# One attention unit's probabilities turned on TensorE for three of four head pairs, and a higher planned price for a DMA of turned blocks

## The chip, the cores and the metric

The kernel runs on one core of one Trainium2 chip. The metric is device time in microseconds (us) of one execution, taken as the median of several timed runs. The engines of the core are TensorE (PE in the profile, with PEld for its weight loads), VectorE (DVE), ScalarE (ACT), GpSimd (POOL) and SyncE (SP), whose queue issues all DMA transfers of this kernel.

## What is computed

Attention with a few global keys and a local window, four sequences of 768 positions, eight heads of 64, and on its output a gated feed-forward layer:

```python
B, H, S, D = q.shape                                   # 4, 8, 768, 64
scores = (1.0 / np.sqrt(D)) * np.matmul(q, k.transpose(0, 1, 3, 2))
rel = pos[:, None] - pos[None, :]
is_global = pos[None, :] < n_global                    # 8
is_local = (rel >= 0) & (rel < n_local)                # 96
dist = np.where(is_global & ~is_local, n_local, np.abs(rel))
scores = np.where(is_global | is_local, scores - slopes * dist, -1e9)
a = softmax(scores)                                    # over the keys
x = np.matmul(a, v)                                    # to [3072, 512]
out = ((x @ w_a) * (x @ w_b)) @ w_out                  # [512, 1536] twice, [1536, 512]
```

All of it is float32.

## The kernel before, in words

**Units.** The 3072 rows are 24 blocks of 128, and these are dealt out to eight units of 4, 2, 3, 3, 3, 3, 3 and 3 blocks (UNITS). A unit has an attention and a feed-forward part. While TensorE works on the feed-forward part of unit u, the attention of unit u+1 is woven in between. Names carry the unit: p15_4 is the second projection (1) of unit 5 for the fourth-numbered piece of the 1536 hidden columns, acc5_0 an output block of unit 5, ps6_3_2 the scores of unit 6, head 3, block 2, and pa6_1 the attention output of unit 6, head pair 1. "Third unit" is unit 2, whose attention lies beside the feed-forward part of unit 1, the shortest of them, with two blocks.

**Feed-forward** (moe, L934 on). For each of twelve pieces of 128 hidden columns: proj makes 24 matmuls into p0 and p1 (each product is three matmuls of split halves, L970), DVE multiplies the two (L1009), ACT and DVE split the result, and back makes nine matmuls (six for two blocks) into acc (L988). In unit 0 the weights are also converted and split on ACT and DVE (load_w), each piece shortly before its first use.

**Attention of units 2 to 7** (attention, L875 on). For each of the 24 pairs of head and block that a unit has: two score matmuls (L902); on DVE the bias and the row minimum (L608); on ACT the exponential and its sum (L624); on DVE two small steps (L639, L646); then the division (L656 on ACT or L658 on DVE). The probabilities must then be turned, since the product with v needs them by keys. Here DVE transposes squares of 32 by 32 (blocks32, L699) into one shared buffer tp, and swap issues 16 DMAs (L713) that move the squares of a whole head pair to their places in pf. The 20 or 24 matmul records with v (values, L730; the profile shows two for each instruction) write pa, and ACT copies it out. tp lies over the wm tile, so the profile calls it wm. tp and pf exist once each.

**Attention of units 0 and 1** (quad). There turn (L673 on) transposes 128 by 128 on TensorE with an identity matrix (L683) into PSUM, and ACT or DVE copies the result to pf or back to t (L410, L412).

**The order.** No instruction has a place written by hand. Each step is recorded as an Op with a due time, what it reads and writes, and a cost on each engine that may run it; Schedule.order then plays a simple machine with these costs, and the order in which steps start there becomes the order on each queue. A swap's 16 DMAs are 16 Ops of cost 480 (ns, dma=480) on the SP queue, and a reader of a DMA's result becomes ready 2300 after its end there (LAGS), plus spare (SPARE = 200 for values). For everything due before the end of unit 1, search tries 400 random shifts of the due times and keeps the best. SLACK says how many of the twelve pieces before the end of a feed-forward part the next attention is due to end: 3.0.

```python
            due = start + (2 * c + 2) * step
            self.swap(due, pf, slot)
            pa = self.bank("psA", f"pa{u}_{c}")
            self.values(due, pl, range(pl.nb), v, probs, pa)
```

Of the kernel before, what the change touches and what calls it, by code (L numbers as in the profile page):

```python
# [25 lines left out]
P = 128  # L26
# [8 lines left out]
PAIRED = 2  # L35
# [4 lines left out]
CHUNKS = 12  # L40
SQ = 32

START = 52000
WLEAD = 6000
LOADLEAD = 8000
SPLITLEAD = 3000
SLACK = 3.0
BACKLOG = 1.0


SPARE = 200.0
PRICE = {"dve": 2.0, "pool": 2.0}


# [155 lines left out]
class Schedule:  # L210
# [16 lines left out]
    def op(self, due, emit, reads=(), writes=(), spare=0.0, port=(), **costs):  # L227


        self.ops.append(Op(len(self.ops), due, costs, emit, reads, writes, spare, port))  # L230
# [18 lines left out]
    def order(self, ops, dues):  # L249
# [28 lines left out]
        def wins(op, e):  # L278
# [3 lines left out]
            for o, c in op.costs.items():  # L282
                at[o] = max(free[o], now) + c * PRICE.get(o, 1.0)
                for due, index, other in ready[o]:
# [77 lines left out]
def pe(n, m=P):  # L362
    return max(n / 2.23 + 2.5, m / 1.2)
# [5 lines left out]
class Fast:  # L369
# [300 lines left out]
                act=act(w) + 100,  # L670
            )

    def turn(self, due, wins, t, pt, pf):  # L673

        nc = self.nc
        starts = []
        for o, w in wins:
            starts += [o] if w == P else [o, o + w - P]
        n = len(starts) * P

        def emit(e):
            for c, o in enumerate(starts):
                nc.tensor.transpose(pt[:, c * P : c * P + P], t[:, o : o + P], self.ident)  # L683

        self.plan.op(due, emit, [t], [pt], pe=len(starts) * 112)
        self.copy(due, lambda: pf[:, :n], lambda: pt[:, :n], n, [pt], [pf], psum=True)

    def blocks32(self, due, w, t, slot, n):

# [14 lines left out]
    def swap(self, due, pf, m):  # L704

        nc, tp, n = self.nc, self.tp, CHUNKS * SQ
        for a in range(P // SQ):
            for b in range(P // SQ):
                out = lambda a=a, b=b: pf[SQ * b : SQ * b + SQ, a * n : a * n + m * SQ]
                src = lambda a=a, b=b: tp[SQ * a : SQ * a + SQ, b * n : b * n + m * SQ]  # L710
                self.plan.op(
                    due,
                    lambda e, out=out, src=src: nc.sync.dma_start(out(), src()),  # L713
                    [tp],
                    [(pf, (a, b))],
                    dma=480,
                )

    def values(self, due, pl, blocks, v, probs, pa):
# [19 lines left out]
        n = sum(len(pl.vslot[i]) for i in blocks)  # L739
        self.plan.op(due, emit, reads, [pa], pe=n * 218 + 290, spare=SPARE if pl.late else 0.0)  # L740

# [133 lines left out]
    def attention(self, u, start, end):  # L875
        nc, pl, op = self.nc, PLANS[u], self.plan.op

        x = [(self.raw0, WIDE + c * MAXQ) for c in range(2)]
        x += [(self.sbuf([P, MAXQ], F32, f"x{c}", f"x{u}_{c}"), 0) for c in range(2, NCC)]
        if u < PAIRED:  # L880
            self.second(x, start, end)
            return x
        step = (end - start) / H
        for c in range(NCC):
            probs = {}
            v = self.fetch_v(u, c, start + (2 * c + 1) * step - LOADLEAD)
            pf = self.sbuf([P, CHUNKS * P], F32, "pf", f"pf{u}_{c}", 1)
            slot = 0
            for s in range(2):
                h = 2 * c + s  # L890
                due = start + h * step
                raw = self.fetch(u, h, due - LOADLEAD)
                qh, ql, kk = self.split(u, h, due - SPLITLEAD, raw)
                for i in range(pl.nb):
                    due = start + h * step + (i + 1) * step / pl.nb
                    k0, w = pl.kwin[i]
                    n = f"{u}_{h}_{i}"
                    ps = self.bank(("psS", "psT")[(pl.nb * h + i) % 2], "ps" + n)

                    def scores(e, i=i, k0=k0, w=w, ps=ps, qh=qh, ql=ql, kk=kk):  # L900
                        for m, q in enumerate((qh, ql)):
                            nc.tensor.matmul(  # L902
                                ps[:, :w],
                                q[:, i * P : i * P + P],
                                kk[:, k0 : k0 + w],
                                start=m == 0,
                                stop=m == 1,
                            )

                    op(due, scores, [qh, ql, kk], [ps], pe=2 * pe(w))  # L910
                    turn = (pl.nb * h + i) % (TBUFS + len(self.spares))
                    if turn < TBUFS:
                        t = self.sbuf([P, 2 * P], F32, "t", "t" + n, TBUFS)
                    else:
                        t = self.spares[turn - TBUFS]
                    sm = self.sbuf([P, 8], F32, "sm", "sm" + n, 6)
                    self.softmax(h, due, [(0, w)], ps, t, sm, [(self.wm, k) for k in range(MBUFS)])
                    chunks = len(pl.vslot[i])
                    self.blocks32(due, w, t, slot, chunks)

                    def get(k, slot=slot, pf=pf):
                        view = pf[:, :].rearrange("p (a m i) -> p m a i", a=P // SQ, m=CHUNKS)
                        return view[:, slot + k]

                    probs[s, i] = (pf, get)
                    slot += chunks
            due = start + (2 * c + 2) * step
            self.swap(due, pf, slot)
            pa = self.bank("psA", f"pa{u}_{c}")
            self.values(due, pl, range(pl.nb), v, probs, pa)  # L930
            self.result(u, c, due, pa, x)
        return x
# [115 lines left out]
    def run(self):  # L1048
        self.open()
        t = START  # L1050
        x = self.first(t - 3000)
# [6 lines left out]
        def ahead(u, t):  # L1058
            xs[u] = self.attention(u, t, t + (NF - SLACK) * steps[u - 1])

# [385 lines left out]
```

## Time and profile before

| | |
|---|---|
| median of 3 runs | 772.8 us (771.91 to 773.62) |
| profiled execution | 769.24 us |
| its span, first to last instruction | 767.5 us |
| PE busy | 719.2 us (94%) |
| DVE busy | 456.4 us (59%) |
| ACT busy | 398.8 us (52%) |
| DMA queue of the kernel | 73.70 MB, 30.5% of 16 engines |

All times of the trace count from the first instruction. A busy time is the union of an engine's instructions; an idle time before an instruction is put down to what came last of what it waited for. PE is an engine with one queue in order: an instruction that waits holds up all behind it.

### The profile page before, as it was taken

What the parts mean: (1) busy time and instruction counts of PE and PEld (TensorE: products, weight loads), DVE (VectorE), ACT (ScalarE), POOL (GpSimd) and SP (SyncE); (2) the same over time, 40 slices, a digit from 0 to 9 for tenths busy, and PEclk for the clock granted to TensorE, in tenths of its full rate; (3) what the DMA queues carried; (4) which work ended last, traced back from release to release, by engine and by line L of the source; (5) the groups of instructions that cost most, each with busy time, mean ns of one, the idle gap of its engine ahead of it and who ended that gap; (6) DMA issues with size and microseconds to landing.
All of it is one profiled execution on the core that took longest, in us unless ns stands there. A gap on an engine that the chain in (4) does not pass through costs nothing.

```text
span 767.5 us, 12583 instructions
## 1 busy us (share of the span) xinstructions
PE 719.2 (94%) x4344; PEld 643.1 (84%) x4344; DVE 456.4 (59%) x1476; ACT 398.8 (52%) x983; POOL 12.7 (2%) x34
## 2 busy tenths in 40 slices
PE   5799999999898999999989999999899999999996
PEld 4568777798888988898879888898888988889996
DVE  6999999867772664465636656266562666322111
ACT  6999877556562653455525456255452655321111
POOL 1000000000000000000000000000000000000000
PEclk9989999999999999999999999999999999999999
DMA  7878010133452133222332333313232232210001
GB/s 285 354 308 353 20 32 30 48 105 97 112 141 84 56 98 100 69 61 83 91 99 82 81 99 96 87 59 82 85 102 69 87 104 61 54 57 8 1 1 45
DMA packets 38520, 74.57 MB, mean 97 GB/s; under 512 B 8497, under 2 KB 21041, under 8 KB 38449
## 3 DMA queue, kind: packets, MB, share of 16 engines
q1 hardware_dynamic: 38448, 73.70, 30.5%
q8 instruction: 36, 0.59, 0.3%
q14 instruction: 36, 0.29, 0.1%
HBM read 50.07 MB, written 6.29 MB: 73 GB/s over the span
## 4 chain that ended last, share of the span: by engine, by line
PE 46%; SPq 26%; DVE 12%; DMA 6%; issue 5%; ACT 4%; DVEq 0%; ACTq 0%
SPq L713 26%; PE p L970 25%; PE acc L988 13%; DMA pf<-wm 6%; PE pa L730 4%; DVE wm L699 2%; DVE kk L420 2%; DVE ql L576 1%; PE ps L777 1%; DVE t L608 1%; PE ps L902 1%; DVE wm L608 1%; PE pt L683 1%; ACT t L624 1%; DVE kk L412 1%
## 5 line engine op out<-in xcount | busy, mean ns | idle before, releaser
L970 PE MATMUL p<-xh,wt 128*128 128x384 f32 (+2 forms) x1488 | 419.1, 339 | 2.7 <-DVE wt L412 1.7
L970 PEld LDWEIGHTS p<-xh,wt 128*128 128x128 f32 x1488 | 271.1, 189 | 17.5 <-issue 3.0
L970 PE MATMUL p<-xl,wt 128*128 128x384 f32 (+2 forms) x816 | 270.5, 341 | 0.5 <-DVE xl L837 0.3
L988 PE MATMUL acc<-wt,hh 128*128 128x512 f32 x576 | 205.3, 397 | 0.0
L970 PEld LDWEIGHTS p<-xl,wt 128*128 128x128 f32 x816 | 153.7, 189 | 10.1 <-DVE xl L837 0.6
L1009 DVE TENSOR_TENSOR raw<-p,raw 128x384 f32<-128x384 f32 (+2 forms) x96 | 53.2, 554 | 136.3 <-PE p L970 123.1
L988 PEld LDWEIGHTS acc<-wt,hh 128*128 128x128 f32 x576 | 108.8, 189 | 21.8 <-issue 2.1
L988 PE MATMUL acc<-wt,hl 128*128 128x512 f32 x288 | 113.6, 394 | 0.0
L410 ACT COPY raw<-p 128x384 f32<-128x384 f32 (+2 forms) x96 | 45.8, 477 | 105.5 <-PE p L970 103.6
L410 ACT CAST hh<-raw 128x384 fp32r<-128x384 f32 (+2 forms) x87 | 44.1, 507 | 56.6 <-DVE raw L1009 55.9
L730 PE MATMUL pa<-pf,v 128*64 128x128 f32 x640 | 43.1, 278 | 30.8 <-DMA pf<-wm 24.9
L730 PEld LDWEIGHTS pa<-pf,v 128*64 128x64 f32 x640 | 35.8, 138 | 40.4 <-issue 33.0
L624 ACT ACTIVATE t<-t,sm 128x232 f32<-128x232 f32 (+2 forms) x120 | 57.1, 480 | 20.3 <-DVE sm L608 19.2
L420 DVE TENSOR_TENSOR hl<-raw,hh 128x384 fp32r<-128x384 f32 (+2 forms) x96 | 53.1, 553 | 19.9 <-ACT hh L410 19.4
L988 PEld LDWEIGHTS acc<-wt,hl 128*128 128x128 f32 x288 | 54.5, 189 | 7.4
L608 DVE CUSTOM_DVE_ANT_0 t<-ps,rel 128x232 f32<-128x232 f32 (+1 forms) x100 | 39.0, 399 | 34.1 <-PE ps L902 32.3
L656 ACT ACTIVATE t<-t,sm 128x232 f32<-128x232 f32 (+2 forms) x86 | 40.4, 485 | 21.0 <-DVE sm L646 16.8
L699 DVE STREAM_TRANSPOSE wm<-t 128x256 f32<-128x256 f32 (+1 forms) x72 | 25.7, 399 | 42.4 <-DMA pf<-wm 39.8
L624 ACT ACTIVATE wm<-wm,sm 128x232 f32<-128x232 f32 (+2 forms) x72 | 34.2, 476 | 18.7 <-DVE sm L608 18.3
L656 ACT ACTIVATE wm<-wm,sm 128x232 f32<-128x232 f32 (+2 forms) x57 | 26.9, 477 | 28.7 <-DVE sm L646 21.1
L420 DVE TENSOR_TENSOR kk<-raw,kk 64x348 fp32r<-64x348 f32 (+1 forms) x82 | 38.5, 470 | 2.5
L902 PE MATMUL ps<-kk,ql 128*128 128x128 f32 (+1 forms) x144 | 39.4, 275 | 0.0
(86 smaller groups left out, 671.6 us busy)
## 6 DMA issues: line engine op xcount, KB each, us to landing
wr<-wts SPq DMA_DIRECT2D x24, 768.0 KB, 10.2
pf<-wm SPq DMA_DIRECT2D x192, 48.0 KB, 1.9
raw<-qkv SPq DMA_DIRECT2D x24, 366.0 KB, 3.1
pf<-wm SPq DMA_DIRECT2D x192, 40.0 KB, 1.9
raw<-qkv SPq DMA_DIRECT2D x24, 314.0 KB, 3.0
v<-qkv SPq DMA_DIRECT2D x16, 384.0 KB, 3.1
out<-o SPq DMA_DIRECT2D x23, 256.0 KB, 2.1
v<-qkv SPq DMA_DIRECT2D x16, 256.0 KB, 2.6
```

Of the source, the lines that this page charges most:

```text
L410: self.nc.scalar.copy(out(), src())
L420: lambda e: self.engine(e).tensor_sub(out(), a(), b()),
L608: lambda e, j=j, o=o, w=w, neg=neg: nc.vector.tensor_tensor_reduce(t[:, o : o + w], ps[:, o : o + w], neg[:, :w], -(2.0 ** -(h + 1)), 3.0e ...
L624: lambda e, j=j, o=o, w=w: nc.scalar.activation(t[:, o : o + w], t[:, o : o + w], AF.Exp, bias=sm[:, j : j + 1], scale=-1.0, accum_out=sm[ ...
L656: nc.scalar.mul(t[:, o : o + w], t[:, o : o + w], r)
L699: nc.vector.transpose(dst, src)
L713: lambda e, out=out, src=src: nc.sync.dma_start(out(), src()),
L730: nc.tensor.matmul(pa[D * s : D * s + D, i * P : i * P + P], v[:, v0 : v0 + D], probs[s, i][1](c), start=c == 0, stop=c == len(slots) - 1,)
L902: nc.tensor.matmul(ps[:, :w], q[:, i * P : i * P + P], kk[:, k0 : k0 + w], start=m == 0, stop=m == 1,)
L970: nc.tensor.matmul(p[:, :T], wt(), b[:, b0 : b0 + T], start=c == 0 and n == 0, stop=c == NCC - 1 and n == 2,)
L988: nc.tensor.matmul(acc[i][:, :], hs[:, i * P : i * P + P], wt(), start=f == 0 and n == 0, stop=f == NF - 1 and n == 2,)
L1009: lambda e, asb=asb, pb=pb: nc.vector.tensor_mul(asb[:, :T], pb[:, :T], asb[:, :T]),
```

## The change

Four things change.

1. In swap each of the 16 DMAs is planned at SWAP = 640 in place of 480. This is a number of the plan alone; the DMAs are the same.
2. SLACK becomes 3.5: the attention of each unit is due half a piece earlier.
3. In unit 2 (SHORT), for the head pairs 0, 2 and 3 (OLD), the six probability blocks of a pair are not transposed by DVE and moved by 16 DMAs, but by TensorE with turn: for each head and block one or two 128 by 128 transposes into bank psT, and a copy to pf. That is ten transposes and six copies a pair. Pair 1 of unit 2 and all pairs of units 3 to 7 keep blocks32 and swap.
4. The scores of these three pairs all use bank psS, where they alternated between psS and psT. turn's Op gets a spare of 200 and writes part of pf from column p0 on.

```diff
+SHORT = PAIRED
+OLD = (0, 2, 3)
...
-SLACK = 3.0
+SLACK = 3.5
...
+SWAP = 640.0
...
-        self.plan.op(due, emit, [t], [pt], pe=len(starts) * 112)
-        self.copy(due, lambda: pf[:, :n], lambda: pt[:, :n], n, [pt], [pf], psum=True)
+        self.plan.op(due, emit, [t], [pt], pe=len(starts) * 112, spare=spare)
+        out = lambda: pf[:, p0 : p0 + n]
+        self.copy(due, out, lambda: pt[:, :n], n, [pt], [(pf, p0)], psum=True)
...
-                    dma=480,
+                    dma=SWAP,
...
+            old = u == SHORT and c in OLD
...
-                    ps = self.bank(("psS", "psT")[(pl.nb * h + i) % 2], "ps" + n)
+                    ps = self.bank(("psS", "psT")[not old and (pl.nb * h + i) % 2], "ps" + n)
...
-                    self.blocks32(due, w, t, slot, chunks)
-
-                    def get(k, slot=slot, pf=pf):
+                    if old:
+                        pt = self.bank("psT", "pt" + n)
+                        self.turn(due, [(0, w)], t, pt, pf, slot * P, SPARE)
+                    else:
+                        self.blocks32(due, w, t, slot, chunks)
+
+                    def get(k, slot=slot, pf=pf, old=old):
+                        if old:
+                            return pf[:, (slot + k) * P : (slot + k + 1) * P]
...
-            self.swap(due, pf, slot)
+            if not old:
+                self.swap(due, pf, slot)
```

Since all instructions are placed by the plan, nearly every place moves a little. Three places follow. The lines of the changed file are a few higher: L902 becomes L909, L970 L984, L988 L1002, L730 L736, L683 L688, L420 L425, L608 L613.

**Place 1, TensorE, a head pair with a swap (unit 6, pair 1).** First before, from the last scores of the pair (ps6_3_2) to its product with v (pa6_1):

```order
L902 MATMUL ps6_3_2_5878<-kk6_3_5665,qh6_3_5663 128x232
L902 MATMUL ps6_3_2_5878<-kk6_3_5665,ql6_3_5673 128x232
L970 MATMUL p15_4_5835<-xh5_5481,wt4_1_933 128x384
...
L988 MATMUL acc5_0_5626<-wt5_1_1015,hl5_5_6003 128x512
L988 MATMUL acc5_0_5626<-wt5_1_1015,hh5_5_5993 128x512
L730 MATMUL pa6_1_6060<-pf6_1_5940,v6_1_5459 64x128 x10
L988 MATMUL acc5_1_5633<-wt5_1_1015,hh5_5_5993 128x512
```

and now:

```order
L909 MATMUL ps6_3_2_5832<-kk6_3_5665,qh6_3_5663 128x232
L909 MATMUL ps6_3_2_5832<-kk6_3_5665,ql6_3_5673 128x232
L984 MATMUL p05_4_5826<-xh5_5481,wt4_0_913 128x384
...
L984 MATMUL p15_6_6031<-xl5_5491,wt6_1_1098 128x384
L984 MATMUL p15_6_6031<-xh5_5481,wt6_1_1098 128x384
L736 MATMUL pa6_1_6058<-pf6_1_5909,v6_1_5465 64x128 x10
...
L909 MATMUL ps6_5_2_6079<-kk6_5_5850,qh6_5_5848 128x232
```

Between the scores and the product with v there stood 82 matmuls: 51 of L970, 21 of L988 and 10 of scores. Now there are 104: 66 of L970 (now L984), 18 of L988 (now L1002), 10 of scores, and the 10 instructions of the pair before, pa6_0.

**Place 2, TensorE, the third unit, pair 0.** Before, its block transposes stand on VectorE, between steps of the feed-forward part of unit 1:

```order
L658 TENSOR_SCALAR wm_505<-wm_505,sm2_1_2_1721 128x232
L639 TENSOR_SCALAR sm2_2_0_1756<-sm2_2_0_1756 128x1
L699 STREAM_TRANSPOSE wm_505<-wm_505 128x2x4x32
L420 TENSOR_TENSOR hl1_1_1794<-raw0_88,hh1_1_1782 128x256
L646 RECIPROCAL sm2_2_0_1756<-sm2_2_0_1756 128x1
```

Now the same block (head 1, block 2) is turned on TensorE, pt2_1_2, a few matmuls ahead of the pair's product with v:

```order
L984 MATMUL p11_2_1793<-xh1_1579,wt2_1_741 128x256
L688 MATMUL pt2_1_2_1823<-ident_93,wm_440 128x128 x2
L984 MATMUL p01_3_1827<-xh1_1579,wt3_0_830 128x256
L984 MATMUL p01_3_1827<-xl1_1594,wt3_0_830 128x256
...
L909 MATMUL ps2_2_1_1844<-kk2_2_1690,ql2_2_1725 128x256
L736 MATMUL pa2_0_1849<-pf2_0_1615,v2_0_1253 64x128 x10
```

The 16 DMAs of the pair are gone from the SP queue, the transposes are on TensorE's, and the copies to pf are on ACT's and DVE's.

**Place 3, VectorE, the weights of unit 0's piece 5.** wt5_0 is the first half of that piece's weights; its last write is a TENSOR_TENSOR (L420, now L425). Before:

```order
L498 ISA wm_505<-wr5_0_585,wm_505 128x1536
L459 TENSOR_SCALAR wm_505<-wm_505 128x768
L608 ISA t0_1_1_0_978,sm0_1_1_0_979<-ps0_1_1_0_926,rel_70 128x232
...
L420 TENSOR_TENSOR wt5_0_976<-wm_505,wt5_0_976 128x768
L479 SCALAR_TENSOR_TENSOR wm_505<-wr5_1_630,wm_505 128x768
```

and now:

```order
L503 ISA wm_440<-wr5_0_588,wm_440 128x1536
L484 SCALAR_TENSOR_TENSOR wm_440<-wr5_1_631,wm_440 128x768
...
L503 ISA wm_440<-wr5_1_631,wm_440 128x1536
L1023 TENSOR_TENSOR raw0_88<-p10_4_960,raw0_88 128x512
...
L425 TENSOR_TENSOR wt5_0_997<-wm_440,wt5_0_997 128x768
```

The write stood in row 224 of VectorE's order and stands in row 240: two steps for the piece's second half and a multiplication of the feed-forward part have come ahead of it. Its first reader on TensorE (the first matmul of piece 5) is row 292 in both.

More of the change, by code (lines that the diff above doesn't have):

```diff
@@ L671, in softmax, with turn @@
             )
-    def turn(self, due, wins, t, pt, pf):
+    def turn(self, due, wins, t, pt, pf, p0=0, spare=0.0):
         nc = self.nc
```

## The prediction

> **What bounds the kernel now.** I read the page first, then the busy times by stage, then who TensorE waited for. The page:
>
> ```profile
> span 767.5 us, 12583 instructions
> PE 719.2 (94%) x4344; PEld 643.1 (84%) x4344; DVE 456.4 (59%) x1476; ACT 398.8 (52%) x983; POOL 12.7 (2%) x34
> ```
>
> TensorE is busy for 94%, so it is the bound, and the time can only fall by its idle 48 us or by less work on it. Busy time by stage (start, unit 0, unit 1, units 2 to 6, unit 7; the columns are the length, then the busy time and count of PE, PEld, DVE, ACT and POOL, the granted clock, the DMA share and GB/s):
>
> ```profile
> 0.00:60.00 60.00, 46.84 (x305) 34.24 (x306) 49.98 (x183) 51.90 (x129) 2.51 (x20) 0.91 0.82 320
> 60.00:160.00 100.00, 99.88 (x511) 79.35 (x510) 95.97 (x204) 74.65 (x146) 0.00 (x0) 1.00 0.25 86
> 160.00:228.00 68.00, 63.97 (x492) 58.59 (x491) 48.80 (x196) 39.72 (x116) 2.33 (x3) 1.00 0.41 116
> 228.00:690.00 462.00, 436.76 (x2664) 404.05 (x2663) 248.25 (x874) 218.74 (x566) 7.88 (x11) 1.00 0.29 82
> ```
>
> Idle are 13.2 us at the start, 0.1 in unit 0 (where DVE is full as well), 4.0 beside unit 1 and 25.2 after that. TensorE's waits name the last two:
>
> ```profile
> PE pa L730 <- DMA pf<-wm: 24.9, 21, 2.0
> ...
> PE pa L730 <- issue: 3.9, 3, 2.1
> ```
>
> That is 24 waits, one for each head pair of units 2 to 7, all ahead of the product with v: 28.8 us, 1.2 each. (The three put down to "issue" stand at the same instruction.) Why TensorE comes too early is seen in the SP queue and in TensorE's timeline, here for two pairs:
>
> ```profile
> 482.82 10.02 SPq L713 DMA_DIRECT2D pf<-wm  x16
> ...
> 538.51 11.56 SPq L713 DMA_DIRECT2D pf<-wm  x16
> ```
> ```profile
> pf<-wm SPq DMA_DIRECT2D x192, 48.0 KB, 1.9
> ```
> ```profile
> 494.46 1.53 PE L730 MATMUL pa<-pf,v 128*64 128x128 f32 x24 [0.81 <-issue]
> ...
> 551.75 1.31 PE L730 MATMUL pa<-pf,v 128*64 128x128 f32 x20 [2.01 <-DMA pf<-wm]
> ```
>
> Sixteen issues take 10.0 us (0.63 each), at worst 11.6, and the last lands 1.9 us after its issue. The plan before counts 16 x 0.48 + 2.3 + 0.2 (the spare of values) = 10.2 us from the first issue to the product with v. The second pair shows 551.75 - 538.51 = 13.2 us; the first, which is the usual case, 10.0 - 0.6 + 1.9 = 11.3 to the last landing and 494.46 - 482.82 = 11.6 to TensorE's start. So the product stands 1.4 to 3 us too early in the queue, and in an in-order queue all feed-forward work behind it waits.
>
> **Part 1, the price of 640: -27.8 us.** The plan now counts 16 x 0.64 + 2.3 + 0.2 = 12.7 us, 1.1 more than the usual 11.6 and 0.5 less than the worst. What was put between can be counted in the order, with these durations:
>
> ```profile
> 476.28 0.39 PE L988 MATMUL acc<-wt,hh 128*128 128x512 f32 x1
> 476.51 0.34 PE L970 MATMUL p<-xh,wt 128*128 128x384 f32 x1
> 476.69 0.34 PE L970 MATMUL p<-xl,wt 128*128 128x384 f32 x1
> ...
> 478.40 1.53 PE L730 MATMUL pa<-pf,v 128*64 128x128 f32 x24 [0.98 <-DMA pf<-wm]
> ```
>
> From start to start an L988 matmul takes 0.23 us, an L970 one 0.175; the 1.31 us of a pair's product above hold ten instructions, 0.13 each. At place 1 the work between last scores and product grows by 15 x 0.175 - 3 x 0.23 + 10 x 0.13 = 3.2 us, against the wait of 2.0. Counted so for all twenty pairs of units 3 to 7, the growth is 1.8 to 4.9 us for nineteen, each more than that pair's wait. For pair 0 of unit 3 it is -0.2, but this pair's block transposes no longer wait for a swap of unit 2 to free tp. The other way in which a wait could come back is pf: pair 1's swap may not start until TensorE has read pair 0's pf. From the end of pa6_0 to pa6_1 the new order has 13.4 us of matmuls; needed are 0.4 for a load of v ahead in the SP queue and 11.6 to 13.2 for the swap. That is enough by a margin of 1.4, or short by 0.2. So of 28.8 us I let 1.0 remain: -27.8; bounds -28.8 and -22.8 (6 us left, 0.3 a pair).
>
> One of these waits also lowered the clock:
>
> ```profile
> 243.18 1.94 PE L730 MATMUL pa<-pf,v 128*64 128x128 f32 x24 [2.10 <-issue]
> ```
> ```profile
> 240.00:244.00 4.00, 1.90 (x22) 1.61 (x22) 0.96 (x3) 0.48 (x1) 0.00 (x0) 1.00 0.18 49
> 244.20:247.50 3.30, 3.30 (x16) 2.48 (x13) 0.61 (x2) 0.99 (x2) 0.00 (x0) 0.50 0.37 110
> ```
>
> After the idle 2.10 us the granted clock was 0.50 for 3.4 us, which costs 1.7. With the wait goes this: **-1.7** (bounds -1.7 and 0). The Trainium skill, "TensorE: Matmul & The Clock Gate", Part 1, has the clock fall only after an idle window of about 3.4 us; by that this wait was too short and the sum would be 1.7 higher. The trace has the drop right behind the wait, and I take the trace.
>
> **Part 2, the transposes on TensorE: +3.0 us.** Three pairs of ten make 30. Unit 1's are the nearest rows, and all TensorE transposes in one group:
>
> ```profile
> 92.19 1.03 PE L683 MATMUL pt<-ident,t 128*128 128x128 f32 x8
> 92.98 0.94 PE L970 MATMUL p<-xl,wt 128*128 128x512 f32 x3
> ```
> ```profile
> L683 PE MATMUL pt<-ident,t 128*128 128x128 f32 x88 | 14.5, 293 | 2.7 <-DVE sm L646 2.0 <-DVE t L658 0.3 <-ACT t L656 0.2
> ```
>
> Eight take 0.79 us until the next matmul starts: 0.1 each, 3.0 for 30. If ones and twos do not overlap with their neighbours, the whole mean of 0.293 counts: 8.8. I take the lower, since the neighbours are ready. The Trainium skill, "VectorE: DVE Perf Modes", section "The three transpose paths", gives a 128 by 128 transpose on TensorE 390 ns, more than VectorE's 311; by it 30 would cost 11.7 us. The rows show 0.1 in a stream.
>
> The 18 block transposes that DVE loses and the 18 copies that ACT and DVE gain lie beside other work (48.8 and 39.7 us busy of 68 beside unit 1). The 48 DMAs that the SP queue loses, 30 us of issues, free it for loads; TensorE gains by that only its waits, counted above.
>
> **Part 3, new waits at the transposes: +0.5 us.** Each turn stands in TensorE's queue and waits for its block's softmax. Its steps, as grouped in units 1 to 7:
>
> ```profile
> L608 DVE CUSTOM_DVE_ANT_0 t<-ps,rel 128x232 f32<-128x232 f32 x47 | 18.2, 393 | 27.1 <-PE ps L902 26.5
> L624 ACT ACTIVATE t<-t,sm 128x232 f32<-128x232 f32 x48 | 23.4, 487 | 8.1 <-DVE sm L608 7.4
> L624 ACT ACTIVATION_READ_ACCUMULATOR t<-t,sm 128x1 f32 x71 | 13.3, 187 | 0.0
> L639 DVE TENSOR_SCALAR sm<-sm 128x1 f32<-128x1 f32 x139 | 19.9, 145 | 13.1 <-ACT t L624 5.9 <-ACT wm L624 5.4
> L646 DVE RECIPROCAL sm<-sm 128x1 f32<-128x1 f32 x139 | 22.0, 160 | 3.2
> L656 ACT ACTIVATE t<-t,sm 128x232 f32<-128x232 f32 x44 | 21.3, 488 | 15.0 <-DVE sm L646 10.8 <-DVE sm L639 3.7
> ```
>
> Together 1.9 us without queueing. In the new order the matmuls between scores and turn make 3.3 us or more for all 18, over 8 for twelve. Queueing on DVE and ACT can eat the rest for the four under 3.6. I take 0.5; bounds 0 and 4 (1 us for each of four).
>
> **Part 4, unit 0's new order: +1.5 us.** The random search sees other costs, and its result is another order for the first 160 us. Place 3 is where it matters:
>
> ```profile
> 83.64 0.95 DVE L420 TENSOR_TENSOR wt<-wm,wt 128x768 fp32r<-128x768 f32 x1
> ...
> 87.29 0.39 PE L970 MATMUL p<-xh,wt 128*128 128x512 f32 x1
> ```
>
> The weights of piece 5 were ready at 84.6 and used at 87.3: 2.7 us to spare. Now 16 more DVE instructions stand ahead, by the stage's mean (95.97 us for 204, 0.47) up to 7.5 us, by their sizes some 4.8, so TensorE may wait 2. Other pieces lose less or gain. I take 1.5; bounds -1 (the start's 13.2 us idle may shrink) and +4.5. SLACK moves due times alone; its effect is in the counts above, and from a unit's last projection to the next unit's first, where the attention's result must be ready and split, the order has 1.8 us of other matmuls in units 3 to 7, as before. The scores of the three pairs now share one bank, so the next ones wait until DVE has read the last (0.39 us by the row of L608); with more than ten us of matmuls between the six scores of a pair this is hidden, and would cost 0.4 us a score if the next stood right behind.
>
> **Sum.** -27.8 - 1.7 + 3.0 + 0.5 + 1.5 = -24.5 us. The profiled execution took 769.24 us, 1.74 of it around the span of 767.5; it would take 744.7. The median of the runs shown is 772.8, 3.6 above it; I carry the difference over: **748.3 us**.
>
> **The rivals.**
> *The waits move.* pf and tp exist once, so every product that stands later frees pf later, and the next swap starts later; if half of the waits return in this form, 12 us of gain are lost: 760. For it: the margin of 1.4 us above, and swaps of 11.6 us. Against: nineteen of twenty pairs got more cover than they waited. 0.11.
> *Transposes at full length.* 30 x 0.293 instead of 0.1 and the upper bound of new waits: +5.8 + 3.5, 757.6. By the skill's 390 ns alone it would be 757.0, hence the same rival. 0.08.
> *Slower: the turns hold TensorE.* If each of the 18 turns waited for its softmax, from 24.5 / 18 = 1.4 us each on the gain would be gone; at 1.6 us plus the transposes, already counted, it ends at 748.3 + 18 x 1.6 = 777. For it: at the start TensorE did wait 2.0 us once for such a step (the row of L683 above). Against: twelve of the 18 have over 8 us of cover. 0.03.
> *The plan spends the price elsewhere*, and nothing changes: the order at place 1 speaks against it. 0.02.
>
> **How the numbers follow.** The forecast has 0.76. With the terms at their good ends the time is 28.8 + 1.7 - 3.0 + 1.0 = 28.5 below 772.8, 744.3; its own bad end, some of the bounds together, is 755. The range of 743.5 to 757.5 takes in nearly all of the transposes rival and leaves out the waits that move and the slow side. The measurement can tell about 0.2%, 1.5 us. Faster 0.95, same 0.02, slower 0.03.
>
> **What would show it.** Right: TensorE's waits at the product with v fall from 28.8 to under 6 us; 21 swaps with issues of 10 us as before; the transposes in unit 2 add 3 us of TensorE time; no half clock near 244; the stage from 228 to 690 shorter by some 24 us. Wrong: waits for pf of 0.5 us or more in most pairs; waits at the turns (L683, now L688) over 4 us in sum; TensorE idle for weights between 60 and 160.

## The result, and the profile after

| | before | after |
|---|---|---|
| median | 772.36 us (769.02 to 773.62, 4 runs) | 742.12 us (741.50 to 742.48, 4 runs) |
| profiled execution | 769.24 us | 742.13 us |
| its span | 767.5 us | 740.2 us |

The ratio is 0.9614, with a 95% interval of 0.9583 to 0.9645. The change is faster, as forecast, but by more: 30.2 us between the medians and 27.1 between the profiled executions, where 24.5 had been forecast. The time of 742.1 lies 1.4 us below the range that was given (743.5 to 757.5).

The changed kernel's page, its span and the share of each engine:

```profile
span 740.2 us, 12564 instructions
PE 717.2 (97%) x4374; PEld 642.7 (87%) x4374; DVE 458.0 (62%) x1479; ACT 394.9 (53%) x984; POOL 10.5 (1%) x30
```

Its busy times by stage, in the same windows and columns as before:

```profile
0.00:60.00 60.00, 44.83 (x306) 33.04 (x307) 52.02 (x190) 52.82 (x132) 2.04 (x19) 0.97 0.83 321
60.00:160.00 100.00, 100.00 (x513) 79.78 (x512) 89.56 (x175) 67.94 (x128) 1.46 (x2) 1.00 0.25 87
160.00:228.00 68.00, 66.85 (x517) 60.67 (x517) 47.51 (x195) 45.99 (x139) 0.00 (x0) 1.00 0.29 86
228.00:690.00 462.00, 461.42 (x2813) 428.39 (x2812) 261.13 (x907) 219.45 (x571) 7.02 (x9) 1.00 0.29 82
```

From 228 to 690 TensorE was idle for 25.2 us and is now idle for 0.6. The start has 2.0 us more of idle time, 15.2 against 13.2 us, but a granted clock of 0.97 where it was 0.91. All of TensorE's waits over 0.3 us in the changed kernel, in sum, with their count and the longest:

```profile
PE ps L783 <- DVE rel L1335: 5.8, 1, 5.8
PE pt L688 <- ACT t L661: 2.4, 2, 1.7
PE pt L688 <- DVE sm L651: 2.0, 1, 2.0
PE p L984 <- ACT raw L415: 1.9, 2, 1.3
PE p L984 <- DVE wt L417: 1.0, 1, 1.0
PE p L984 <- ACT xl L415: 0.9, 1, 0.9
PE acc L1002 <- ACT hh L415: 0.6, 1, 0.6
PE p L984 <- DVE wt L425: 0.6, 1, 0.6
PE p L984 <- DVE xl L843: 0.4, 1, 0.4
PE pa L736 <- PE pt L688: 0.4, 1, 0.4
PE acc L1002 <- DVE hl L425: 0.4, 1, 0.4
```

The 24 waits for pf, 28.8 us, are gone without a rest: no row names a DMA any more. The pair of place 1 (unit 6, pair 1) shows how. SP queue and TensorE:

```profile
516.35 10.99 SPq L719 DMA_DIRECT2D pf<-wm  x16
```
```profile
529.32 0.33 PE L984 MATMUL p<-xh,wt 128*128 128x384 f32 x1
529.58 1.31 PE L736 MATMUL pa<-pf,v 128*64 128x128 f32 x20
530.83 0.44 PE L984 MATMUL p<-xh,wt 128*128 128x384 f32 x1
```

The 16 issues take 11.0 us, where the same pair's took 11.6 before. The product starts 13.2 us after the first of them, just as it did before, but without a bracket, that is without a wait: projections stood ahead of it until the data were there.

### The profile page after: what moved, and what is told of

Its sections match the earlier page's. It is cut to its first block, busy times and chain, and to the rows that moved or that the text cites. A ratio compares the mean times of both kernels' runs of the same rounds, so it can differ in the third digit from the quotient of the medians.

```text
span 740.2 us, 12564 instructions
## 1 busy us (share of the span) xinstructions
PE 717.2 (97%) x4374; PEld 642.7 (87%) x4374; DVE 458.0 (62%) x1479; ACT 394.9 (53%) x984; POOL 10.5 (1%) x30
## 4 chain that ended last, share of the span: by engine, by line
PE 93%; ACT 3%; DVE 3%; DMA 0%; issue 0%; ACTq 0%
PE p L984 54%; PE acc L1002 27%; PE pa L736 5%; PE ps L909 4%; PE pt L688 1%; PE ps L783 1%; ACT t L629 1%; ACT wr L494 1%; ACT pf L415 1%; DVE t L613 0%; DMA nv<-ns 0%; ACT wm L457 0%; DVE kk L425 0%; ACT t L661 0%; DVE t L663 0%
## 5 line engine op out<-in xcount | busy, mean ns | idle before, releaser
L984 PE MATMUL p<-xh,wt 128*128 128x384 f32 (+2 forms) x1488 | 421.1, 339 | 3.5 <-ACT raw L415 1.9
L984 PEld LDWEIGHTS p<-xh,wt 128*128 128x128 f32 x1488 | 271.8, 189 | 17.8 <-issue 3.7
L984 PE MATMUL p<-xl,wt 128*128 128x384 f32 (+2 forms) x816 | 270.2, 341 | 1.2 <-ACT xl L415 0.9
L1002 PE MATMUL acc<-wt,hh 128*128 128x512 f32 x576 | 203.4, 395 | 0.6 <-ACT hh L415 0.6
L984 PEld LDWEIGHTS p<-xl,wt 128*128 128x128 f32 x816 | 153.8, 189 | 10.5 <-ACT xl L415 1.2
L1002 PEld LDWEIGHTS acc<-wt,hh 128*128 128x128 f32 x576 | 108.2, 188 | 21.4 <-issue 1.1
L1002 PE MATMUL acc<-wt,hl 128*128 128x512 f32 x288 | 113.2, 393 | 0.4 <-DVE hl L425 0.4
L425 DVE TENSOR_TENSOR hl<-raw,hh 128x384 fp32r<-128x384 f32 (+2 forms) x96 | 53.3, 556 | 24.8 <-ACT hh L415 24.2
L629 ACT ACTIVATE t<-t,sm 128x232 f32<-128x232 f32 (+2 forms) x120 | 56.9, 477 | 17.1 <-DVE sm L613 16.1
L1002 PEld LDWEIGHTS acc<-wt,hl 128*128 128x128 f32 x288 | 54.2, 188 | 8.3 <-DVE hl L425 0.7
L613 DVE CUSTOM_DVE_ANT_0 t<-ps,rel 128x232 f32<-128x232 f32 (+1 forms) x100 | 39.1, 400 | 28.2 <-PE ps L909 27.1
L661 ACT ACTIVATE t<-t,sm 128x232 f32<-128x232 f32 (+2 forms) x77 | 36.1, 479 | 18.7 <-DVE sm L651 14.9
L629 ACT ACTIVATE wm<-wm,sm 128x232 f32<-128x232 f32 (+2 forms) x72 | 34.1, 474 | 19.1 <-DVE sm L613 18.4
L661 ACT ACTIVATE wm<-wm,sm 128x232 f32<-128x232 f32 (+2 forms) x66 | 31.3, 478 | 21.0 <-DVE sm L651 13.6
L736 PE MATMUL pa<-pf,v 128*64 128x128 f32 x640 | 41.8, 277 | 0.6 <-PE pt L688 0.4
L736 PEld LDWEIGHTS pa<-pf,v 128*64 128x64 f32 x640 | 34.4, 137 | 8.4 <-issue 6.6
L425 DVE TENSOR_TENSOR kk<-raw,kk 64x244 fp32r<-64x244 f32 (+1 forms) x86 | 39.9, 464 | 2.6
L909 PE MATMUL ps<-kk,ql 128*128 128x128 f32 (+1 forms) x144 | 39.4, 275 | 0.0
L909 PE MATMUL ps<-kk,qh 128*128 128x128 f32 (+1 forms) x144 | 38.1, 267 | 0.0
```

The source lines that it names most:

```text
L425: lambda e: self.engine(e).tensor_sub(out(), a(), b()),
L613: lambda e, j=j, o=o, w=w, neg=neg: nc.vector.tensor_tensor_reduce(t[:, o : o + w], ps[:, o : o + w], neg[:, :w], -(2.0 ** -(h + 1)), 3.0e ...
L629: lambda e, j=j, o=o, w=w: nc.scalar.activation(t[:, o : o + w], t[:, o : o + w], AF.Exp, bias=sm[:, j : j + 1], scale=-1.0, accum_out=sm[ ...
L661: nc.scalar.mul(t[:, o : o + w], t[:, o : o + w], r)
L736: nc.tensor.matmul(pa[D * s : D * s + D, i * P : i * P + P], v[:, v0 : v0 + D], probs[s, i][1](c), start=c == 0, stop=c == len(slots) - 1,)
L909: nc.tensor.matmul(ps[:, :w], q[:, i * P : i * P + P], kk[:, k0 : k0 + w], start=m == 0, stop=m == 1,)
```

## The experiments

Thirteen orders of the same kernel, each compared with runs of the kernel before on the same chip. For the changed kernel's row its median was 772.4 us (4 runs); for the twelve others, which ran on three chips, it was 770.2 (19 runs), 769.3 (9) and 770.2 us (7).

| kernel | price | turns | SLACK | median, us | ratio to before (95%) |
|---|---|---|---|---|---|
| the changed kernel | 640 | yes | 3.5 | 742.1 | 0.961 (0.958 to 0.965) |
| price_only | 640 | no | 3.0 | 743.7 | 0.965 (0.961 to 0.968) |
| turn_only | 480 | yes | 3.0 | 770.5 | 0.999 (0.996 to 1.002) |
| no_turn | 640 | no | 3.5 | 742.3 | 0.963 (0.960 to 0.967) |
| price_480 | 480 | yes | 3.5 | 774.5 | 1.005 (1.003 to 1.007) |
| slack_3 | 640 | yes | 3.0 | 742.7 | 0.966 (0.963 to 0.969) |
| lag_only | 480, delay 4860 | no | 3.0 | 745.8 | 0.970 (0.967 to 0.973) |
| price_400 | 400 | yes | 3.5 | 823.6 | 1.070 (1.065 to 1.075) |
| price_560 | 560 | yes | 3.5 | 742.6 | 0.964 (0.960 to 0.968) |
| price_800 | 800 | yes | 3.5 | 741.9 | 0.963 (0.959 to 0.967) |
| seed2 | 640 | yes | 3.5 | 740.5 | 0.962 (0.957 to 0.966) |
| after_t0 | 640 | yes, no search | 3.5 | 744.2 | 0.968 (0.966 to 0.970) |
| no_turn_t0 | 640 | no, no search | 3.5 | 748.6 | 0.974 (0.972 to 0.976) |

### The parts one by one

**price_only**, the kernel before with one number changed:

```diff
-                    dma=480,
+                    dma=640,
```

> The kernel before with the planned price of a swap's DMA at 640 and nothing else: no turns in the third unit, SLACK 3.0. Theory T (a wait at the product with v is what is missing between the matmuls planned behind the last scores and the 15 to 17 us that softmax, block transposes and 16 DMAs take): the order now has 16.6 to 19.2 us there for units 3 to 7, before 14.0 to 15.4, so all twenty waits go, in unit 2 as well (19 to 22 us), and no transposes are added: 27 to 31 us faster than before, 742 to 746. Rival C (the third unit is the tight one, its late swaps hold up all that follows, and the turns there bring the gain): under 10 us faster.

743.7 us: the price alone brings the gain. From unit 2 on no wait at the product is left in its profile; its longest waits are of the start:

```profile
PE ps L777 <- DVE rel L1321: 5.7, 1, 5.7
PE pt L683 <- DVE t L658: 4.7, 2, 4.4
PE pt L683 <- DVE sm L646: 2.0, 1, 2.0
```

**turn_only**, the changed kernel without the price and the SLACK:

```diff
-SLACK = 3.5
+SLACK = 3.0
-SWAP = 640.0
+SWAP = 480.0
```

> The changed kernel with the price back at 480 and SLACK at 3.0: only the turns of three pairs of the third unit are left of the change. Theory T: the order of units 3 to 7 has the same 14.0 to 15.4 us of matmuls between last scores and product as before, so their waits stay at about 25 us; the third unit loses 3 us of waits and gains 3 us of transposes: within 4 us of before. Rival C (the third unit holds up the rest): over 12 us faster.

770.5 us, no difference from before. The waits stay, now for 21 pairs:

```profile
PE pa L736 <- DMA pf<-wm: 21.9, 16, 2.7
...
PE pa L736 <- issue: 4.2, 5, 1.4
```

Rival C, by which the third unit holds up all that follows, has fallen with these two.

**no_turn**, the changed kernel with all pairs swapped:

```diff
-OLD = (0, 2, 3)
+OLD = ()
```

> The changed kernel (640, SLACK 3.5) with the turns taken out again: all 24 pairs swap. Theory T: no waits at the product in units 3 to 7, as in the changed kernel, and 3 us of transposes less; in unit 2 the planned 19 to 21 us cover the swaps too: 1 to 4 us faster than the changed kernel, 738 to 741, unless the attention of unit 2 then ends too late for unit 2's first projection. Rival C: over 10 us slower than the changed kernel.

742.3 us, the same as the changed kernel. That misses the expected 738 to 741: the three microseconds that the transposes cost do not come back. after_t0 and no_turn_t0 ask why.

**price_480**, the changed kernel with the old price:

```diff
-SWAP = 640.0
+SWAP = 480.0
```

> The changed kernel with the price back at 480 (turns and SLACK 3.5 kept). Theory T: 14.0 to 15.6 us of matmuls between last scores and product in units 3 to 7, as before, so some 22 us of the waits come back: 764 to 770. Rival S (the earlier due time of SLACK 3.5 gives the cover): within 5 us of the changed kernel, 740 to 747.

774.5 us. The waits come back, as theory T has it, and the earlier due time gives nothing by itself, so rival S falls; but the time is 4.5 us above the range. It is also 4.0 us above turn_only, measured on the same chip with 10 runs each, from which it differs in SLACK alone: with the old price, SLACK 3.5 costs something. The waits are 25.4 + 3.4 = 28.8 us, for 21 pairs as much as before for 24:

```profile
PE pa L736 <- DMA pf<-wm: 25.4, 16, 3.0
PE ps L783 <- DVE rel L1335: 6.0, 1, 6.0
PE pa L736 <- issue: 3.4, 5, 0.9
```

In turn_only they are 26.1 us. The clock was halved here in three windows between 160 and 700 us, in turn_only in one. One of the three is behind the longest wait. Here is that wait, and the granted clock (after the four busy times and POOL's) in the stretch with it, right after it and then:

```profile
442.22 0.95 PE L736 MATMUL pa<-pf,v 128*64 128x128 f32 x13 [3.02 <-DMA pf<-wm]
```
```profile
441.50:443.50 2.00, 1.28 (x24) 1.31 (x24) 1.40 (x6) 0.00 (x0) 0.00 (x0) 1.00 0.69 200
443.60:446.90 3.30, 3.30 (x14) 3.16 (x11) 2.77 (x9) 0.97 (x2) 0.00 (x0) 0.50 0.50 131
447.00:450.00 3.00, 3.00 (x17) 2.79 (x17) 1.15 (x5) 1.56 (x4) 0.00 (x0) 1.00 0.56 176
```

**slack_3**, the changed kernel with the old SLACK:

```diff
-SLACK = 3.5
+SLACK = 3.0
```

> The changed kernel with SLACK back at 3.0 (640 and the turns kept). Theory T: the waits at the product stay away (16.6 to 19.2 us of matmuls), so within 3 us of the changed kernel: 740 to 745. Rival: the attention then ends too late for the next unit's first projection, which has only 2.8 us of matmuls behind the attention's end in place of 4.0; if that is not enough, TensorE idles some 1 us at each of five borders: 746 to 749.

742.7 us: at the price of 640 SLACK makes no difference that these runs can tell.

### What the price must cover

**lag_only**, the kernel before with the same 2.56 us planned as a delay of the result:

```diff
-LAGS = {"pe": 200.0, "act": 270.0, "dve": 230.0, "pool": 290.0, "dma": 2300.0}
+LAGS = {"pe": 200.0, "act": 270.0, "dve": 230.0, "pool": 290.0, "dma": 4860.0}
```

> The kernel before with the price at 480, no turns and SLACK 3.0, but the plan's delay of every DMA result raised from 2300 to 4860, which is the 2.56 us that 16 x 160 add. Theory T (only the sum from first issue to product counts): the order has the same 16.6 to 19.2 us of matmuls as with the price at 640 alone, the waits go: 740 to 746, within 3 us of price_only. Rival P (the price must be on each DMA, since the SP queue itself is what is misjudged: loads behind the swap come late): over 8 us slower than price_only.

745.8 us, 2.1 above price_only on another chip; from unit 2 on no wait at the product is left. What counts is the sum of the matmuls put ahead of the product, not that the price sits on each DMA. The 2.1 us more lie before 250 us: from there to 690 TensorE is busy for 439.96 of 440 us in both.

**price_400, price_560 and price_800** are the changed kernel with SWAP at these numbers.

> The changed kernel with the price at 560: 15.6 to 18.2 us of matmuls. Theory T: waits of under 0.6 us in a third of the pairs, below 5 us in sum, no window of half clock between 160 and 700: 742 to 747, runs within 3 us of each other. Rival (the price must reach the measured 630 ns for the gain): half of the gain, 755 or more.

742.6 us. Waits are left at seven products, but short ones, 3.2 us in sum:

```profile
PE pa L736 <- issue: 1.7, 3, 0.9
...
PE pa L736 <- PE p L984: 1.0, 2, 0.6
...
PE pa L736 <- DMA pf<-wm: 0.6, 2, 0.4
```

> The changed kernel with the price at 800: 19 to 27 us of matmuls, well over need. Theory T: no waits at the product, and nothing more to gain: within 3 us of the changed kernel, 740 to 745, as long as the attention still ends before the next unit's first projection. Rival (a product that stands later holds pf and tp longer, the rival of the waits that move): waits come back somewhere behind, over 5 us slower than the changed kernel.

741.9 us: more than enough costs nothing here. The rival of the waits that move, from the prediction, is not seen at any price from 560 to 800.

> The changed kernel with the price at 400. The order of units 3 to 7 has 12.5 to 13.9 us of matmuls behind the last scores, against the 15.0 to 16.9 that were needed at 480. Theory W (waits of about 1.8 us and more at times halve the clock for a 3.4 us window, at 1.7 us each, and this is why runs with waits differ by up to 8 us): waits of 2 to 3.5 us, in sum 45 to 60 us, and 5 or more windows of half clock between 160 and 700 us; 800 to 825, a clock below that of price_480 and a wide spread of runs. Rival Y (the windows have nothing to do with the waits): at most two such windows, and the time is 742 plus the waits.

823.6 us, 53 above the kernel before on its chip. Its waits, and its busy time from 228 to 770 with the clock:

```profile
PE pa L736 <- DMA pf<-wm: 43.7, 17, 4.0
PE pa L736 <- issue: 10.6, 5, 2.7
```
```profile
228.00:770.00 542.00, 489.37 (x2847) 452.74 (x2846) 267.15 (x930) 222.49 (x582) 4.53 (x6) 0.96 0.25 71
```

54.1 us of waits at 21 products (one more of 0.2 us in these rows is of the start), and a mean clock of 0.96. Between 160 and 700 us the clock record has 13 stretches at 0.50, one of them two windows long, so 14 windows of 3.41 us, each of which costs half its length: 23.9 us. Waits and windows make 78.0 us. The profiled execution took 819.67 us, 77.5 more than the changed kernel's; unit 1's feed-forward part begins 1.7 us later in it, so the two agree to some 2 us. Theory W holds: each of the 13 stretches begins between 0.6 us before and 1.4 us behind the end of a wait of 1.9 to 4.0 us at the product; the other eight waits, 1.7 to 2.7 us long, have none. The starts lie whole multiples of 3.41 us apart (from 196.43 to 251.05 it is 16 of them), and where a wait falls on this grid decides. Here are two waits of 2.70 us, and the stretches of the grid in which they lie:

```profile
277.73 1.13 PE L736 MATMUL pa<-pf,v 128*64 128x128 f32 x13 [2.70 <-DMA pf<-wm]
```
```profile
583.95 1.31 PE L736 MATMUL pa<-pf,v 128*64 128x128 f32 x20 [2.70 <-DMA pf<-wm]
```
```profile
274.94:278.35 3.41, 0.71 (x13) 0.65 (x14) 0.64 (x2) 0.00 (x0) 0.00 (x0) 1.00 0.46 120
278.40:281.70 3.30, 3.30 (x22) 2.97 (x19) 1.96 (x11) 2.15 (x7) 0.00 (x0) 0.50 0.26 61
...
582.14:585.55 3.41, 1.60 (x22) 1.46 (x23) 1.62 (x6) 0.08 (x1) 0.00 (x0) 1.00 0.47 136
585.60:588.90 3.30, 3.30 (x22) 3.30 (x21) 1.95 (x9) 1.86 (x7) 0.00 (x0) 1.00 0.27 79
```

The first lies whole in one stretch of the grid, which is idle for 2.70 us, and the clock is halved in the next. The second is cut into 0.89 and 1.81 us, and the clock stays. With the traces of all fourteen kernels laid on their grids, from 160 us to the last matmul, the clock went from full to half after each of the 17 stretches that were idle for 2.06 us or more, after none that was idle for 1.75 or less, and after two of the six between. In the first 60 us the split is not as clean (in seed2 the clock fell behind a stretch idle for 1.41 us).

### What the turns do, and the luck of the start

**after_t0 and no_turn_t0** are the changed kernel and no_turn without the random search, so that both have the same order for the first 160 us:

```diff
-TRIES = 400
+TRIES = 0
```

> The changed kernel without the random search (TRIES 0), so that its order up to the start of unit 1's feed-forward part is the same, row by row, as that of no_turn_t0. To be read against that one: the difference is the turns of the third unit alone. Theory U (30 transposes cost TensorE 3 us and the swaps that they replace cost nothing once the price is right): 2 to 4 us slower than no_turn_t0. Rival V (the swaps of the third unit leave as much idle time as the transposes cost): within 1 us. Against the changed kernel: 0 to 6 us slower, as the start is not searched.

> The changed kernel without the turns (all pairs swap) and without the random search. Theory U: 2 to 4 us faster than after_t0. Rival V: within 1 us of it. The order gives its pair 0 of unit 3 only 14.7 us of matmuls behind the last scores, so one wait of 1 us may be left there.

744.2 and 748.6 us. Theory U and rival V both fall: with the turns the kernel is faster by 4.4 us, though TensorE has 3 us more to do. In no_turn_t0 TensorE waits at the border of units 1 and 2 for VectorE, which is full there with the block transposes among other work, and the clock is halved for three windows:

```profile
228.72 0.34 PE L909 MATMUL ps<-kk,qh 128*128 128x232 f32 x1 [2.41 <-DVE sm L613]
```
```profile
226.00:229.20 3.20, 0.77 (x4) 0.42 (x4) 3.04 (x12) 2.64 (x10) 1.15 (x1) 1.00 0.25 65
229.40:239.50 10.10, 9.16 (x43) 8.45 (x44) 9.40 (x40) 7.87 (x23) 0.93 (x1) 0.50 0.74 249
```

VectorE is busy for 3.04 of 3.20 us in the stretch with the wait. The waits from 228 to 234 are 3.6 us, the half clock costs 5.1, and the transposes saved give back 3.0: 5.7, against 4.9 between the two profiled spans (747.9 and 743.0). With the search, no_turn has an order without this place. That it is still not 3 us faster than the changed kernel lies for the larger part in its start: its unit 1 begins the feed-forward part at 156.4 us, the changed kernel's at 154.5, and the short waits after that are 0.6 us more. So the turns take away a tight place that another order avoids too. That it is the block transposes that VectorE is late with is argued from its full stretch, and not tried apart.

**seed2** is the changed kernel with another seed:

```diff
-        rnd = random.Random(1)
+        rnd = random.Random(2)
```

> The changed kernel with another seed of the random search: units 3 to 7 keep their order, the first 230 us get another. Theory T: the start and unit 0 decide a few us by luck, in idle time before 60 us and in windows of half clock there: 740 to 746. If the changed kernel's own order of the start was a lucky one, slower than it by 1 to 4 us.

740.5 us, the lowest median of all, but the ratio to before on its chip, 0.962, is the changed kernel's. In thirteen profiles the first matmul of unit 1's feed-forward part starts between 152.7 us (seed2) and 158.2 (lag_only); in the kernel before it is 156.1, in the changed kernel 154.5. The order of the start is worth some 3 us either way.

## Why the prediction was wrong, by its own steps

The mechanism and the direction were right; the time was missed by 6.2 us (748.3 against 742.1), and the range lay too high. The sum is off by 2.6 of this, and one step behind it by 3.6.

*The step that failed: "I carry the difference over".* The profiled execution of before was 3.6 us faster than the median of the three runs, and the prediction took these 3.6 us as something that the changed kernel would have as well. It has not: its four runs lie within 1.0 us of each other, the profiled one among them. Without this step the same sum gives 744.7 us, and its good end 769.24 - 28.5 = 740.7, so the measured 742.1 lies between the two.

The 3.6 us were for the most part a matter of those three runs. A fourth run beside them took 769.0 us, and in the experiments the medians of 19, 9 and 7 runs of before are 770.2, 769.3 and 770.2 us, at most 1.0 above the profiled execution. So part of the 30.2 us between the medians comes from a high median of before, and the 27.1 us between the profiled executions are the better measure of the gain. Why those three runs were slow is open. A chip that slows every kernel does not fit: the changed kernel's runs there are no slower than its near variants elsewhere (742.1 against 742.7 in slack_3, 742.6 in price_560 and 741.9 in price_800).

The clock is one part of what varies. The runs of before on one chip spread from 767.3 to 775.3 us (19 runs), with a mean clock from 0.985 to 0.997, and the slower ones tend to the lower clock (a correlation of -0.76). Kernels with waits at the product spread by 4.4 (price_480, 10 runs), 5.5 (price_400, 4) and 5.7 us (turn_only, 10), those without them, or with short ones, by 1.0 to 2.3 (4 or 5 runs each). The grid of clock windows lies differently in each trace (its first stretch begins 0.15 to 3.25 us after the first instruction), so the same waits may cost a window in one run and none in another; this is argued, as one run of each kernel was profiled. But the clock does not explain the 3.6 us: the profiled execution's own clock, 0.990, is no higher than those of the other runs (0.992 is the median of the 19). And in price_480 time and clock do not go together (-0.06). The term "one of these waits also lowered the clock, -1.7" was right for the one execution that was profiled. As an estimate from the stretches above, three of its 24 waits (1.90, 2.01 and 2.10 us) were long enough to cost a window if they fall whole into one stretch, so a range of 0 to 5.1 us would have been the better term.

*Part 1, the price, -27.8.* It came to -28.8: nothing was left of the waits where 1.0 had been left. The counts of matmuls behind the last scores were the right tool: they put no pair short at 640, seven just short at 560 (3.2 us in sum), and all 21 short at 480 and 400 (28.8 and 54.1 us). The clock window near 244 is gone, as forecast.

*Part 2, the transposes, +3.0.* The row of TensorE's timeline in the third unit bears out the price of 0.1 us each: two transposes and the projection behind them

```profile
163.67 0.38 PE L688 MATMUL pt<-ident,t 128*128 128x128 f32 x2
163.80 0.36 PE L984 MATMUL p<-xh,wt 128*128 128x256 f32 x1
164.00 0.28 PE L984 MATMUL p<-xl,wt 128*128 128x256 f32 x1
```

take 0.33 us to the next start, where the projection alone takes 0.12 (164.00 to 164.12): 0.21 for two. The 390 ns that "VectorE: DVE Perf Modes", section "The three transpose paths", in the Trainium skill gives for a bf16 transpose are not what these float32 ones cost here. "TensorE gains by that only its waits" was too short: the swaps that go also relieve VectorE at the border of units 1 and 2, which no term had (no_turn_t0).

*Part 3, new waits at the turns, +0.5.* There is one of 0.1 us in unit 2; the rows of L688 above are of the start. Three short waits elsewhere were in no term, 1.6 us together: the two rows of L1002, at the border of units 1 and 2, and 0.6 of the 1.9 us of L984 for raw, at 663 us.

*Part 4, the start's order, +1.5.* This term had the wrong sign. Unit 1's feed-forward part begins 1.6 us earlier than before, not 1.5 later. No wait for weights came between 60 and 160 us: TensorE is busy for 100.00 of 100. The extra VectorE instructions at place 3 did make the write later, but by 2.2 us (it ends at 86.8 us) and not by the 4.8 or more that their sizes gave, as the order ahead of it differs too; the piece's first matmul starts at 87.5, where it was 87.3. And the waits of the start fell so that the clock was at half for 3.4 us there where it had been for 10.2 (0.97 against 0.91 in the first 60 us), which is worth 3.4 us against the 2.0 us more of idle time. With the parts as they came out the sum is -28.8 - 1.7 + 3.0 + 0.1 + 1.6 - 1.6 = -27.4, against 27.1 measured. Part 4 is luck: the thirteen orders begin unit 1's feed-forward part anywhere between 152.7 and 158.2 us.

*The rivals.* The waits that move (760) were refuted by price_800, the dearer transposes (757.6) by the timeline above, the turns that hold TensorE (777) by their waits. That the plan spends the price elsewhere was refuted by the profile after.

## What to carry to other kernels

In a queue that runs in order, an instruction placed too early costs its wait in full. A planner's price for what it waits for is worth checking against the trace before anything else, and it is enough to count the work that the order puts in between: too high a price cost nothing here from 560 to 800, too low a price 32 us at 480 and 81 at 400. Where short waits can halve the clock, the waits' sum is not their whole price. One profiled execution and the median of three runs can differ by the luck of either; the difference belongs to those runs of the kernel before, and is to be explained or measured with more runs, not carried over.

## What the runs showed of the hardware

- A wait of TensorE of 1.8 to 4.0 us may be followed at once by a window of 3.41 us at a granted clock of 0.50, at 1.7 us each; in price_400 it was so for 13 of 21 waits, in price_480 for three, in turn_only and in the kernel before for one each. From 160 us on, what decided was how much of one stretch of a 3.41 us grid was idle: 2.06 us or more always did it in these traces, 1.75 or less never. "TensorE: Matmul & The Clock Gate", Part 1, of the Trainium skill lets the clock fall only after an idle window of about 3.4 us; the traces show it fall after windows that were idle for 1.77 us and more.
- Issuing a DMA of 32 partitions by 320 or 384 elements takes the SP queue 0.63 us, 16 of them 10.0 us and up to 11.6.
